# Spacers of 32 bytes between the input weight tiles of a fused attention and two-MoE kernel

## The chip, the cores and the metric

One NeuronCore of a Trainium2 chip runs the whole kernel. The metric is the device time of one execution in microseconds; before the change the median of 3 runs is 587.91 us (587.55 to 588.61). A profile is one execution recorded by the hardware profiler.

## What is computed

The reference chains a decayed linear attention and two dense feed-forward layers, all in float32:

```
attn: q, k, v of (2, 8, 768, 64); per head a decay lam; blocks with a causal decay mask and a running state
x   = attn output as (1536, 512)
layer 1: h = x @ w_in (512 x 2048);  g = h * clip(h + 3, 0, 6) / 6;  x = g @ w_out (2048 x 512)
layer 2: h = x @ w_in2;  g = (a0 + a1 h + a2 h^2 + a3 h^3) / (1 + |b0||h| + |b1| h^2 + 1e-6);  out = g @ w_out2
```

q, k and v are float32, the weights arrive as float64 (two 32-bit words an element), and the output is float32 (1536, 512).

## The kernel before

**Products.** Each float32 operand of the two layers is held as a pair of fp32r tiles, a rounded high part and the rest (names end in h and l). A product is three matmuls: high by high, high by low, low by high. The weights of a layer are cut into 16 slices f of 128 hidden columns; the tokens into 3 blocks tb of 512. Slice f has four weight tiles of 2048 bytes in each partition: `wih`, `wil` (input weights, four pieces kk of 128 columns) and `woh`, `wol` (output weights). The second layer's weights overwrite the first's in the same tiles.

**Steps.** There are 96 steps s: two layers, three blocks, sixteen slices. Step s has 24 matmuls of 512 moving columns. `mm1(s)` (L226, L228, L230) makes the hidden block in the PSUM bank `hb` with 12 of them: a piece of `wih` or `wil` is the stationary operand, a piece of the activation tiles `xh` or `xl` (2048 bytes each) the moving one. `mm2(s)` (L245) adds the slice to the four accumulators `acc` with 12 more: in layer 1 pieces of `woh`, `wol` are stationary and the hidden tiles `gh`, `gl` move; in layer 2 pieces of `gh`, `gl` are stationary and `woh`, `wol` move. The order of mm1 and mm2 is the list `turns`; a step's mm2 comes two or three steps after its mm1. In the last twelve steps `gh` and `gl` live in the input weight tiles of slices 0 to 11, which are no longer needed (`g_tiles`). Every matmul has its own weight load (PEld in the profile), which runs beside the matmul ahead of it.

**Around it.** ScalarE, VectorE and GpSimd turn the weights of the next slice from float64 into the two fp32r tiles (`conv_c` to `conv_h`) and make the hidden activations (`act1`, `act2`, `act_fin`). The attention is interleaved with the first steps; its tiles lie in the pool `ap`.

**Where the tiles lie.** A pool is a stretch of each partition's SBUF and its tiles follow each other in the order of their `tile` calls. From the left end stand `const`, then `wp` with the input weights of slices 0 to 4 and the output weights of slices 0 to 8 (`w_tiles(wp, range(EARLY), range(EOUT))`), then the activations `xp`, the scratch pools `tp` and `rp`, and the hidden tiles `gp`. Behind them comes `pp` for the first loads, and when that is closed `wr` takes its place with the input weights of slices 5 to 10. From the right end stand `side`, an area of 704 bytes that nothing reads or writes (`spare`), and then `ap`; when the attention is over `wq` takes its place with the input weights of slices 11 to 15 and the output weights of slices 9 to 15. In this layout all of these weight tiles, the activation tiles and the hidden tiles begin at the same byte modulo 2048, namely 1312: `wih0` at 1312, `xh0` at 58656, `gh` at 138528, `wih5` at 154912, `wih11` at 179488, `woh9` at 199968.

Of the kernel before, what the change touches and what calls it, by code (L numbers as in the profile page):

```python
# [8 lines left out]
F32 = mybir.dt.float32  # L9
# [21 lines left out]
def fused_kernel(  # L31
# [45 lines left out]

    def w_tiles(pool, ins, outs):
        for f in ins:
            W["in", f] = [pool.tile([128, KD, 128], F32R, name=f"wi{x}{f}") for x in "hl"]  # L80
        for f in outs:
            W["out", f] = [pool.tile([128, DM], F32R, name=f"wo{x}{f}") for x in "hl"]


    side = ctx.enter_context(tc.tile_pool(name="side", bufs=1, side="right"))
    side.tile([128, 176], F32, name="spare")
    EARLY, EIN, EOUT = 5, 11, 9
    w_tiles(wp, range(EARLY), range(EOUT))
    pre = ExitStack()
    pp = pre.enter_context(tc.tile_pool(name="pp", bufs=1))  # L90
# [228 lines left out]
    with ExitStack() as actx:  # L319
# [129 lines left out]
        with tc.manual_schedule():  # L449
# [84 lines left out]
            for s in range(att_steps):  # L534
                c = CPT + s
                j = s + 3
                if s == 0:
# [21 lines left out]
                    pre.close()  # L559
                    wr = ctx.enter_context(tc.tile_pool(name="wr", bufs=1))  # L560
                    w_tiles(wr, range(EARLY, EIN), ())
                else:
                    mm1(s + 1)
# [30 lines left out]

    wq = ctx.enter_context(tc.tile_pool(name="wq", bufs=1, side="right"))
    w_tiles(wq, range(EIN, NF), range(EOUT, NF))
    W2AT = N1 - NF
    with tc.manual_schedule():
# [100 lines left out]
```

## Time and profile before

| what | value |
|---|---|
| median of 3 runs | 587.91 us |
| span of the profiled execution, first to last instruction | 586.0 us |
| PE (matmul) busy | 580.1 us, 99% of the span |
| PEld (weight load) busy | 475.4 us, 81% |
| DVE / ACT / POOL busy | 429.8 / 385.4 / 361.2 us |
| matmuls | 3117, of which 2304 belong to the 96 steps |

The profile has no other time for that execution than its span, so sums are made against 586.0 us and then carried over to the median, which lies 1.91 us higher. A matmul row's duration is latency, not rate: matmuls are pipelined and overlap. The rate is read from the distance between two starts.

### The profile page before, as it was taken

Reading aid. Unit: us, or ns where it says so; the run is one execution under the profiler, and the core shown is the slowest. Engines: PE = TensorE matmul, PEld = TensorE weight load, DVE = VectorE, ACT = ScalarE, POOL = GpSimd, SP = SyncE. Lnnn points to the kernel's source line nnn. Section 1 sums busy time; section 2 is a strip of 40 time slices with the busy share of each in tenths; the row PEclk is TensorE's granted clock in tenths of the full one; section 3 lists DMA queues with packets and bytes.
Section 4 is the critical chain, followed back from the end, with each engine's and each line's share of the span. In section 5 each row is a group of like instructions: output and inputs, shape, how many; then the busy total and the mean of one; then the engine's idle time right before and its main releaser. Section 6 shows DMA issues by size and latency. Waiting matters only on the chain.

```text
span 586.0 us, 8507 instructions
## 1 busy us (share of the span) xinstructions
PE 580.1 (99%) x3117; PEld 475.4 (81%) x3117; DVE 429.8 (73%) x478; ACT 385.4 (66%) x650; POOL 361.2 (62%) x290
## 2 busy tenths in 40 slices
PE   8999999999999999999999999999999999999997
PEld 6777787888888888888888888888888888888885
DVE  6797676887211012688888999999998888999991
ACT  3686656786322223677778888888876677877771
POOL 3665757566221222476667778788776767777771
PEclk9999999999999999999999999999999999999999
DMA  9998673553000000456563001000100000100001
GB/s 184 258 263 225 160 229 126 161 162 107 1 0 1 0 1 1 165 194 182 177 196 128 2 0 37 1 1 1 73 1 0 1 1 1 72 1 0 2 1 72
DMA packets 61674, 46.69 MB, mean 80 GB/s; under 512 B 39488, under 2 KB 56128, under 8 KB 61632
## 3 DMA queue, kind: packets, MB, share of 16 engines
q1 hardware_dynamic: 61344, 46.02, 27.8%
q8 instruction: 24, 0.39, 0.3%
q10 hardware_dynamic: 288, 0.14, 0.1%
q14 instruction: 18, 0.15, 0.1%
HBM read 43.00 MB, written 3.15 MB: 79 GB/s over the span
## 4 chain that ended last, share of the span: by engine, by line
PE 96%; SPq 2%; DMA 1%; issue 0%; DVE 0%; ACT 0%
PE acc L245 45%; PE hb L226 15%; PE hb L228 15%; PE hb L230 15%; SPq L348 2%; DMA vn<-in_v_dram 1%; PE Y L391 1%; PE X L424 1%; PE Y L424 1%; PE X L413 1%; PE X L391 1%; PE hb L418 1%; PE Y L369 1%; PE X L364 1%; PE acc L391 0%; PE acc L418 0%
## 5 line engine op out<-in xcount | busy, mean ns | idle before, releaser
L314 DVE RECIPROCAL Y<-tb 128x512 f32<-128x512 f32 x48 | 161.3, 3361 | 1.6
L291 POOL TENSOR_TENSOR gl<-td,gh 128x512 fp32r<-128x512 f32 x84 | 109.1, 1298 | 82.4 <-ACT gh L290 82.4
L226 PE MATMUL hb<-xh,wih 128*128 128x512 f32 x384 | 103.8, 392 | 0.0
L228 PE MATMUL hb<-xh,wil 128*128 128x512 f32 x384 | 102.7, 389 | 0.0
L230 PE MATMUL hb<-xl,wih 128*128 128x512 f32 x384 | 102.7, 389 | 0.0
L305 POOL TENSOR_TENSOR tc<-ta,tc 128x512 f32<-128x512 f32 x48 | 62.3, 1297 | 55.0 <-ACT tc L302 55.0
L281 DVE SCALAR_TENSOR_TENSOR td<-tc,hb 128x512 f32<-128x512 f32 x48 | 32.8, 684 | 79.8 <-ACT tc L278 79.8
L230 PEld LDWEIGHTS hb<-xl,wih 128*128 128x128 f32 x384 | 72.1, 188 | 15.1
L228 PEld LDWEIGHTS hb<-xh,wil 128*128 128x128 f32 x384 | 72.1, 188 | 15.1
L226 PEld LDWEIGHTS hb<-xh,wih 128*128 128x128 f32 x384 | 71.4, 188 | 15.9 <-issue 1.4
L245 PE MATMUL acc<-gh,woh 128*128 128x512 f32 x192 | 76.1, 396 | 0.0
L245 PE MATMUL acc<-gl,woh 128*128 128x512 f32 x192 | 74.9, 390 | 0.0
L245 PE MATMUL acc<-gh,wol 128*128 128x512 f32 x192 | 74.8, 390 | 0.0
L278 ACT ACTIVATE tc<-hb,c 128x512 f32<-128x512 f32 x48 | 32.8, 684 | 60.6 <-PE hb L230 60.4
L290 ACT CAST gh<-td 128x512 fp32r<-128x512 f32 x84 | 52.0, 619 | 25.4 <-DVE td L281 13.5
L306 POOL TENSOR_TENSOR td<-td,tc 128x512 f32<-128x512 f32 x48 | 64.4, 1341 | 3.8
L218 POOL TENSOR_TENSOR wil<-ta,wih 128x512 fp32r<-128x512 f32 x32 | 41.5, 1296 | 28.2 <-ACT wih L217 28.2
L299 ACT ACTIVATE X<-hb,b_sb 128x512 f32<-128x512 f32 x48 | 31.8, 662 | 39.0 <-PE hb L230 36.2
L245 PE MATMUL acc<-woh,gh 128*128 128x512 f32 x144 | 56.0, 389 | 0.0
L245 PE MATMUL acc<-wol,gh 128*128 128x512 f32 x144 | 56.0, 389 | 0.0
L245 PE MATMUL acc<-woh,gl 128*128 128x512 f32 x144 | 56.0, 389 | 0.0
L218 POOL TENSOR_TENSOR wol<-tb,woh 128x512 fp32r<-128x512 f32 x29 | 38.4, 1326 | 14.0 <-ACT woh L217 13.4
(124 smaller groups left out, 1013.2 us busy)
## 6 DMA issues: line engine op xcount, KB each, us to landing
raw<-in_moe_w_in_dram SPq DMA_DIRECT2D x32, 512.0 KB, 4.1
raw<-in_moe_w_out_dram SPq DMA_DIRECT2D x32, 512.0 KB, 4.7
qn<-in_q_dram SPq DMA_DIRECT2D x24, 128.0 KB, 3.8
kn<-in_k_dram SPq DMA_DIRECT2D x24, 128.0 KB, 3.6
vn<-in_v_dram SPq DMA_DIRECT2D x12, 256.0 KB, 5.1
out_dram<-raw SPq DMA_DIRECT2D x11, 256.0 KB, 2.2
out_dram<-raw ACTq DMA_DIRECT2D x1, 128.0 KB, 1.8
out_dram<-raw SPq DMA_DIRECT2D x1, 128.0 KB, 1.8
```

Of the source, the lines that this page charges most:

```text
L218: nc.gpsimd.tensor_tensor(lo, x, hi.bitcast(F32), op=ALU.subtract)
L226: nc.tensor.matmul(h, lhsT=ih[:, kk, :], rhs=xh[tb][:, kk, :], start=kk == 0, stop=False)
L228: nc.tensor.matmul(h, lhsT=il[:, kk, :], rhs=xh[tb][:, kk, :], start=False, stop=False)
L230: nc.tensor.matmul(h, lhsT=ih[:, kk, :], rhs=xl[tb][:, kk, :], start=False, stop=kk == KD - 1)
L245: nc.tensor.matmul(acc[d], lhsT=l, rhs=r, start=st and i == 0, stop=sp and i == 2)
L278: nc.scalar.activation(t, h, AF.Relu, bias=c3)
L281: nc.vector.scalar_tensor_tensor(out=g, in0=t, scalar=6.0, in1=h, op0=ALU.min, op1=ALU.mult)
L290: nc.scalar.copy(gh, g)
L291: nc.gpsimd.tensor_tensor(gl, g, gh.bitcast(F32), op=ALU.subtract)
L305: nc.gpsimd.tensor_tensor(b1, h2, b1, op=ALU.mult)
L306: nc.gpsimd.tensor_tensor(a1, a1, b1, op=ALU.add)
L314: nc.vector.reciprocal(Y, q1)
```

## The change

```diff
@@ -77,13 +77,13 @@
     def w_tiles(pool, ins, outs):
         for f in ins:
+            if f:
+                pool.tile([128, 8], F32, name=f"step{f}")
             W["in", f] = [pool.tile([128, KD, 128], F32R, name=f"wi{x}{f}") for x in "hl"]
         for f in outs:
             W["out", f] = [pool.tile([128, DM], F32R, name=f"wo{x}{f}") for x in "hl"]
 
 
-    side = ctx.enter_context(tc.tile_pool(name="side", bufs=1, side="right"))
-    side.tile([128, 176], F32, name="spare")
     EARLY, EIN, EOUT = 5, 11, 9
```

Ahead of each slice's pair of input weight tiles but the first, an unused tile of 8 float32 (32 bytes) is placed; nothing reads or writes it. The area of 704 bytes at the right end is gone. No instruction is added, removed or moved: on all five engines the changed program has the same instructions in the same order with the same waits; only addresses differ. The addresses of the changed program, as starts modulo 2048 against those of `xh`, `xl`, `gh` and `gl` (all at 1440 now, 128 higher than before, since four spacers stand ahead of them):

| tiles | start against activations, bytes |
|---|---|
| input weights f = 0, 1, 2, 3, 4 | -128, -96, -64, -32, 0 |
| input weights f = 5, 6, 7, 8, 9, 10 | +32, +64, +96, +128, +160, +192 |
| input weights f = 11, 12, 13, 14, 15 | +448, +480, +512, +544, +576 |
| output weights f = 0 to 8 | 0 |
| output weights f = 9 to 15 | +576 |

Before the change every entry of this table is 0.

## Rows read from the trace of the kernel before

**Rows 1.** The page: the span and its first part, busy time by engine.
```profile
span 586.0 us, 8507 instructions
...
PE 580.1 (99%) x3117; PEld 475.4 (81%) x3117; DVE 429.8 (73%) x478; ACT 385.4 (66%) x650; POOL 361.2 (62%) x290
```

**Rows 2.** The waits of PE: who it waited for, total us, times, longest.
```profile
PE Y L477 <- DVE warm L467: 1.2, 1, 1.2
PE acc L418 <- DMA vn<-in_v_dram: 0.6, 1, 0.6
PE acc L391 <- ACT kT L370: 0.2, 1, 0.2
```

**Rows 3.** Busy time by stage; columns as in the first line.
```profile
core 0: us, PE busy (x) PEld busy (x) DVE busy (x) ACT busy (x) POOL busy (x), PEclk, DMA share, GB/s
...
26.30:103.30 77.00, 77.00 (x697) 60.78 (x698) 59.02 (x98) 52.39 (x100) 50.60 (x43) 1.00 0.75 201
103.30:329.30 226.00, 226.00 (x997) 187.12 (x998) 125.66 (x183) 129.89 (x227) 110.42 (x86) 1.00 0.31 96
329.30:490.00 160.70, 160.70 (x710) 133.07 (x709) 150.65 (x106) 125.03 (x197) 122.45 (x95) 1.00 0.03 11
```

**Rows 4.** PE in order of time, a step of layer 1: start us, us, what.
```profile
301.90 0.39 PE L245 MATMUL acc<-gh,woh 128*128 128x512 f32 x1
...
304.62 1.07 PE L226 MATMUL hb<-xh,wih 128*128 128x512 f32 x4
305.53 1.07 PE L228 MATMUL hb<-xh,wil 128*128 128x512 f32 x4
306.44 1.07 PE L230 MATMUL hb<-xl,wih 128*128 128x512 f32 x4
307.34 0.39 PE L245 MATMUL acc<-gh,woh 128*128 128x512 f32 x1
```

**Rows 5.** PE in order of time, a step of layer 2.
```profile
494.34 0.39 PE L245 MATMUL acc<-woh,gh 128*128 128x512 f32 x1
...
497.06 1.07 PE L226 MATMUL hb<-xh,wih 128*128 128x512 f32 x4
...
499.78 0.39 PE L245 MATMUL acc<-woh,gh 128*128 128x512 f32 x1
```

**Rows 6.** PE in order of time among the attention, first stretch.
```profile
31.27 1.19 PE L226 MATMUL hb<-xh,wih 128*128 128x512 f32 x4
32.30 1.08 PE L228 MATMUL hb<-xh,wil 128*128 128x512 f32 x4
33.21 1.07 PE L230 MATMUL hb<-xl,wih 128*128 128x512 f32 x4
34.12 1.07 PE L226 MATMUL hb<-xh,wih 128*128 128x512 f32 x4
```

**Rows 7.** PE in order of time among the attention, later stretches.
```profile
40.96 0.40 PE L245 MATMUL acc<-gl,woh 128*128 128x512 f32 x1
41.20 0.39 PE L245 MATMUL acc<-gh,woh 128*128 128x512 f32 x1
...
44.65 1.08 PE L228 MATMUL hb<-xh,wil 128*128 128x512 f32 x4
45.57 1.08 PE L230 MATMUL hb<-xl,wih 128*128 128x512 f32 x4
46.49 0.38 PE L364 MATMUL X<-ident,qn 128*128 128x128 f32 x2
```

**Rows 8.** PE in order of time, bf16 matmuls at the start.
```profile
6.20 0.38 PE L477 MATMUL Y<-warm 128*128 128x512 bf16 x1
6.42 0.60 PE L369 MATMUL hb<-ident,kn 128*128 128x128 f32 x4
```

**Rows 9.** Line 226's instructions: duration ns min/median/max, first and last start us.
```profile
L226 PEld LDWEIGHTS hb<-xh,wih x384: 186/188/189, 26.2 to 563.5; 128*128 128x128 f32 x192
L226 PE MATMUL hb<-xh,wih x384: 389/389/499, 26.2 to 563.7; 128*128 128x512 f32 x192
```

## The prediction

> **What bounds the kernel now.** I read the first part of the page first: the matmul engine is busy 580.1 of 586.0 us [rows 1]. Then the waits: PE waited 2.0 us in the whole execution, 1.2 + 0.6 + 0.2, each of them once [rows 2]. By stage, PE is busy for every one of the 77.0, 226.0 and 160.7 us between 26.3 and 490.0 us, at a granted clock of 1.00, which is the level of 2.4 GHz, while VectorE, ScalarE and GpSimd each have idle time in all three [rows 3]. So no engine and no transfer holds PE up; the time is the number of matmuls times the distance between their starts, and only a change of that distance can move it.
>
> That distance is the thing to measure. Between 301.90 and 307.34 us one step of layer 1 passes, 24 matmuls of 512 columns in 5.44 us, 226.7 ns each; the three groups of mm1 take 0.91, 0.91 and 0.90 us for four matmuls, so mm1 and mm2 run at one rate [rows 4]. In layer 2, where stationary and moving operands have changed places in mm2, the step from 494.34 to 499.78 us takes 5.44 us again [rows 5]. The steps hold 96 x 24 = 2304 matmuls; at 226.7 ns they are 522 us, nine tenths of the span.
>
> Two observations say that 226.7 ns is not simply the length of the operand. First, 512 columns at one a cycle of 2.4 GHz are 213.3 ns, and a bf16 matmul of the same size at the start has 0.22 us to the next start [rows 8]. So there are some 7 to 13 ns in each fp32r matmul that the columns do not explain, up to 2304 x 13.3 = 31 us in all. Second, the distance is not quite constant. Just after attention work it is longer: from 44.65 to 46.49 us eight matmuls of mm1 take 1.84 us, 230 ns each, and one in mm2 takes 0.24 us to two digits [rows 7]. It then settles: from 32.30 to 33.21 us it is 227.5 ns, and from 33.21 to 34.12 us 227.5 ns again to that precision [rows 6], and in the undisturbed stages it stays at 226.7. Something in how the weight load and the moving stream meet depends on how they stand to each other in time. Whether it also depends on their addresses, no row shows: every weight, activation and hidden tile of the steps begins at the same byte modulo 2048.
>
> **The change part by part.** No instruction is added or removed and no wait changes, so nothing is queued behind anything new. The spacers are neither read nor written: zero instructions, 0 us. The order of the DMAs and their sizes is the same; that their destinations lie 128 to 704 bytes further on could matter only to landing times, and after 26.3 us PE waits for no transfer [rows 2, 3]. The operands of ScalarE, VectorE and GpSimd move too; a few per cent more on any of them would go into idle time of 18 us in 77, 96 in 226 or 10 in 161 on the busiest of them [rows 3], so that is priced at nothing, and the cover is thinnest in layer 2, where VectorE has 10.05 us over some 30 steps, about 0.34 us a step.
>
> What is left is the address relation of the two reads of PE. It changes for these matmuls: in mm1 all slices but f = 4, so 90 of 96 steps with 12 matmuls, 1080; in mm2 the slices 9 to 15, 42 steps with 12, 504; and in the last twelve steps, where the hidden tiles lie in input weight tiles, four more (slices 4 to 7) with 12, 48. That is 1632 of 2304. The effect on one of them is not shown by a row of before, and I bound it from both sides. The best case is the bare column time, 213.3 ns, 13.3 less than now; the nearest measured row on that side is the bf16 matmul at 0.22 us, 7 ns less. The worst case is the 0.24 us of the disturbed mm2, 13 ns more; the nearest group on that side is the 230 ns after attention, 3.3 ns more. In the sum these are 1632 x 13.3 = 21.8 us less, 1632 x 7 = 11.4 us less, 1632 x 13 = 21.2 us more and 1632 x 3.3 = 5.4 us more. The value I take for the forecast is 0, for two reasons that rows give. The steady distance is the same whichever tiles stand against each other: pieces kk of one weight tile lie 512 bytes apart, and mm1 and mm2 and both layers pair different tiles in different regions, yet all come out at 226.7 ns [rows 4, 5]; so a dependence could only be on an offset smaller than 512 bytes. And the weight load itself takes 186 to 189 ns over all 384 instances of line 226, those after attention work among them [rows 9]; a load that collided with the stream more in one case than in another would be expected to spread further. The sum is then 586.0 + 0 = 586.0 us for the profiled execution, and with the 1.91 us that the median lies above it, 587.9 us.
>
> Here a page can be weighed. The rows show two distances for the same operands, 226.7 and 230 ns [rows 4, 7]. The Trainium skill (SBUF — State Buffer, Who interferes with whom) gives the matrix engine two independent read ports, one for the moving operand and one for weight loads, and says that it never waits on anyone. By that rule addresses play no part, the change is worth 0, and the time is 587.9 us; the trace agrees in the constancy of the undisturbed stages and does not agree in the disturbed ones, which the rule leaves unexplained.
>
> **The rivals.** *Slower: the settled state is lost.* The steady 226.7 ns is reached only after some matmuls at 230 ns or more; if it rests on the two streams starting at the same offset, slices at other offsets settle at another value, or are thrown out of it at each border between mm1 and mm2, where the offset jumps in the changed layout by up to 576 bytes and never did before. For it: nearly all of the disturbed distances are above the steady one [rows 6, 7], so another relation is more likely worse than better. Against it: the constancy named above. The price is the 3.3 ns: 1080 x 3.3 = 3.6 us if mm1 alone suffers, 591.5 us, and 5.4 us for all 1632, 593.3 us; with the 0.24 us row it would be 609. It decides as soon as the mean distance over the 1632 rises by 0.7 ns (1.2 us).
>
> *Faster: the equal offset is what costs the extra.* If the surplus over the columns is the two reads meeting in the same place because they begin at the same place, other offsets remove it, wholly or in part. For it: the surplus exists and is in each matmul [rows 4, 8]. Against it: bf16 matmuls also read both operands from one tile at one offset, and their surplus is smaller [rows 8]. At 7 ns for the 1080 of mm1 the gain is 7.6 us, 580.4 us; for all 1632 it is 11.4 us, 576.5 us; at the bare column time 566.1 us.
>
> The Trainium skill (TensorE: Matmul & The Clock Gate, Back-to-back issue gap) puts a stream of 512 columns at 512/2.4 + 2.5 = 215.8 ns. The bf16 row agrees and the fp32r rows do not; if offsets brought the 1632 matmuls down to it, the estimate would be 1632 x 10.9 = 17.8 us less, 570.1 us.
>
> *The change does less than it says.* Slice 4 keeps offset 0, and so do the output weights 0 to 8, since the activation tiles are shifted along. With an effect that depends only on whether a start is a multiple of 64 bytes, the even and the odd slices would part and half of mm1 would move: 540 x 3.3 = 1.8 us or 540 x 7 = 3.8 us, 589.7 or 584.1 us. These sit inside the two rivals and have no chance of their own.
>
> **How the numbers follow.** A measurement of this kernel can tell about 0.2%, 1.2 us, from no change. No dependence on the address: 0.38, 587.9 us, 586.7 to 589.1. The settled state lost: 0.34, 589.1 to 609, mostly 590 to 596. The equal offset was the cost: 0.28, 566 to 586.7, mostly 576 to 586. These are faster 0.28, same 0.38, slower 0.34. The likeliest single case gives the time. A range of 8 in 10 must reach into both rivals: from 577, which leaves out the case in which nearly every changed matmul gains fully (about 0.09), to 596, which leaves out losses of over 5 ns a matmul (about 0.1). The likeliest case alone has 587.0 to 588.9.
>
> **What would show it.** In the changed profile, the distance of 24 matmuls in a step decides everything: 5.44 us for every slice f means no dependence; a distance that differs from step to step in a pattern with period 16, equal in the three blocks and both layers, shows the address at work, and its sign by slice says which rival holds, with slice 4 as the control that must stay at 0.91 us for four matmuls of mm1. PE must still be 99% busy with the same waits. The prediction is wrong if the span leaves 584.8 to 587.2 us; my account of it is wrong if PE shows new waits, because then the time went through another engine and not through the distance of the matmuls.

## The result, and the profile after

The changed kernel takes 596.79 us (median of 4 runs, 596.49 to 597.09) against 587.89 us for the kernel before on the same chip: a ratio of 1.015, 95% interval 1.0136 to 1.0165, slower by 8.9 us. The forecast was 587.9 us with a range from 577 to 596; the time lies above it, on the side of the slower rival.

| what | before | after |
|---|---|---|
| median | 587.89 us | 596.79 us |
| span of the profiled execution | 586.0 us | 595.1 us |
| PE busy | 580.1 us | 589.7 us |
| PEld busy | 475.4 us | 475.9 us |

The page of the changed kernel, its span and busy time by engine; it answers to [rows 1]:

```profile
span 595.1 us, 8507 instructions
...
PE 589.7 (99%) x3117; PEld 475.9 (80%) x3117; DVE 431.3 (72%) x478; ACT 385.5 (65%) x650; POOL 361.5 (61%) x290
```

The instructions are the same in number; the span grew by 9.1 us and PE's busy time by 9.6 us, while the busy time of the others moved by 1.5 us at most. The waits of PE in the changed kernel, which answer to [rows 2], have not grown:

```profile
PE Y L477 <- DVE warm L467: 1.3, 1, 1.3
PE acc L391 <- ACT kT L370: 0.2, 1, 0.2
PE acc L418 <- DMA vn<-in_v_dram: 0.2, 1, 0.2
```

So no other engine and no transfer holds PE up. What changed is the distance between matmuls. PE in order of time in layer 1 of the changed kernel, mm1 of slices 4, 5, 6 and 11, each with the start of what follows it where it is shown; the rows answer to [rows 4]:

```profile
253.18 1.07 PE L226 MATMUL hb<-xh,wih 128*128 128x512 f32 x4
254.09 1.07 PE L228 MATMUL hb<-xh,wil 128*128 128x512 f32 x4
254.99 1.07 PE L230 MATMUL hb<-xl,wih 128*128 128x512 f32 x4
255.90 0.39 PE L245 MATMUL acc<-gh,woh 128*128 128x512 f32 x1
...
258.63 1.09 PE L226 MATMUL hb<-xh,wih 128*128 128x512 f32 x4
259.55 1.10 PE L228 MATMUL hb<-xh,wil 128*128 128x512 f32 x4
260.49 1.10 PE L230 MATMUL hb<-xl,wih 128*128 128x512 f32 x4
...
264.14 1.10 PE L226 MATMUL hb<-xh,wih 128*128 128x512 f32 x4
265.08 1.09 PE L228 MATMUL hb<-xh,wil 128*128 128x512 f32 x4
266.01 1.09 PE L230 MATMUL hb<-xl,wih 128*128 128x512 f32 x4
...
291.82 1.08 PE L226 MATMUL hb<-xh,wih 128*128 128x512 f32 x4
292.73 1.08 PE L228 MATMUL hb<-xh,wil 128*128 128x512 f32 x4
293.65 1.07 PE L230 MATMUL hb<-xl,wih 128*128 128x512 f32 x4
```

Slice 4, whose weights still stand at offset 0, takes 2.72 us for its twelve matmuls (253.18 to 255.90), as before. Slice 5 at +32 takes 0.94 us for four (259.55 to 260.49), slice 6 at +64 takes 0.93 (265.08 to 266.01), slice 11 at +448 takes 0.92 (292.73 to 293.65), against 0.91 at offset 0. The mean distance of the twelve, from the starts in the trace, repeats by slice. Here it stands for the second block of layer 1 beside the offset:

```
slice   0     1     2     3     4     5     6     7     8     9     10    11    12    13    14    15
offset  -128  -96   -64   -32   0     +32   +64   +96   +128  +160  +192  +448  +480  +512  +544  +576
mm1 ns  231.9 233.3 229.4 232.7 226.7 232.8 233.2 234.0 233.0 233.2 229.0 228.8 233.1 229.2 233.1 233.3
```

The third block of layer 1 has the same numbers within 0.1 ns. Summed over the starts of both traces, mm1 has become 5.5 us longer and mm2 3.7 us, together the 9.1 us of the span to rounding. In mm2, the slices 9 to 15 (+576 in layer 1) carry 2.8 us and the slices 0 to 8 carry 0.9 us. Of this 0.9, slices 4 to 7 of the last block, whose hidden tiles lie in input weight tiles, carry 0.25 us; the other 0.6 us fall on matmuls that kept offset 0: the first of them after a disturbed mm1 still run at 224 to 237 ns before they settle at 226.7.

### The profile page after: what moved, and what is told of

Read it like the earlier page. It is cut to its first block, busy times and chain, and to the rows that moved or that the text cites. A ratio compares the mean times of both kernels' runs of the same rounds, so it can differ in the third digit from the quotient of the medians.

```text
span 595.1 us, 8507 instructions
## 1 busy us (share of the span) xinstructions
PE 589.7 (99%) x3117; PEld 475.9 (80%) x3117; DVE 431.3 (72%) x478; ACT 385.5 (65%) x650; POOL 361.5 (61%) x290
## 4 chain that ended last, share of the span: by engine, by line
PE 96%; SPq 2%; DMA 1%; issue 0%; DVE 0%; ACT 0%
PE acc L245 45%; PE hb L226 15%; PE hb L228 15%; PE hb L230 15%; SPq L348 2%; DMA vn<-in_v_dram 1%; PE Y L391 1%; PE X L424 1%; PE Y L424 1%; PE X L413 1%; PE X L391 1%; PE hb L418 1%; PE X L364 1%; PE Y L369 1%; PE acc L391 0%; PE acc L418 0%
## 5 line engine op out<-in xcount | busy, mean ns | idle before, releaser
L226 PE MATMUL hb<-xh,wih 128*128 128x512 f32 x384 | 105.6, 396 | 0.0
L228 PE MATMUL hb<-xh,wil 128*128 128x512 f32 x384 | 104.7, 394 | 0.0
L230 PE MATMUL hb<-xl,wih 128*128 128x512 f32 x384 | 104.4, 393 | 0.0
```

The lines of the kernel that those rows point to most:

```text
L226: nc.tensor.matmul(h, lhsT=ih[:, kk, :], rhs=xh[tb][:, kk, :], start=kk == 0, stop=False)
L228: nc.tensor.matmul(h, lhsT=il[:, kk, :], rhs=xh[tb][:, kk, :], start=False, stop=False)
L230: nc.tensor.matmul(h, lhsT=ih[:, kk, :], rhs=xl[tb][:, kk, :], start=False, stop=kk == KD - 1)
```

## The experiments

Three theories stood against each other. **A:** each offset between the stationary and the moving start has a steady distance of its own. **B:** only the jump of the offset from one group of matmuls to the next costs. **C:** something else that moved, such as the tiles at the right end, is the cause.

### map1: the offset alone

A kernel of its own, which leaves out the computation and issues groups of N = 32 matmuls; `m` and `d` are the moving and the stationary offset in bytes, `c` the stationary columns (the branch for bf16 is left out here):

```
for g, (kind, m, d, c) in enumerate(plan()):
    ...
        l, r = (far if kind == "far" else sta)[:, d // 4 : d // 4 + c], mov[:, m // 4 : m // 4 + 512]
    for i in range(N):
        nc.tensor.matmul(acc[g % 2][0:c, :], lhsT=l, rhs=r, start=True, stop=True)
```

> This kernel leaves out the whole computation: it issues groups of 32 matmuls of 512 fp32r columns with one stationary and one moving tile, and from group to group only the byte offset of the stationary start against the moving start changes (0 to 1024 in steps of 32, then 4 to 60 in steps of 4, then both starts shifted together by 32, 64 and 256, then fewer stationary columns, a stationary tile 98 KB further on, and bf16). Theory A, each offset has a steady distance of its own that repeats every 512 bytes: 226.7 ns at 0, 512 and 1024, about 229 at 192 and 448, 232 to 234 at 32, 64, 96, 128 and 160, the same again from 512 to 1024, and 226.7 when both starts move together. Theory B, only the jump of the offset between groups of matmuls costs: after at most 10 matmuls every group is at 226.7 ns. Theory C, the address relation is not the cause (other engines' addresses are): all groups at 226.7 from the start.

Measured, as mean distance of the last 20 matmuls of a group in ns; the values of 256 to 480, 512 to 736 and 768 to 992 are those of 0 to 224 within 0.1:

```
offset   0      32     64     96     128    160    192    224    256
ns       226.7  233.4  233.4  234.1  232.4  233.2  228.9  233.4  226.7
```

Busy time by stretch in map1, where each stretch reaches from the first start of one group of 32 to that of the next (the columns are stretch, us, PE busy and the matmuls that reach into it, granted clock, DMA share, GB/s). The offsets are 64, 96, 128, 160, 192, 224, 256:

```profile
26.05:33.52 7.47, 7.47 (x34) 1.00 0.01 2
33.52:41.00 7.48, 7.48 (x33) 1.00 0.00 0
41.00:48.43 7.43, 7.43 (x33) 1.00 0.00 0
48.43:55.90 7.47, 7.47 (x34) 1.00 0.00 0
55.90:63.23 7.33, 7.33 (x34) 1.00 0.01 2
63.23:70.69 7.46, 7.46 (x33) 1.00 0.00 0
70.69:77.95 7.26, 7.26 (x33) 1.00 0.00 0
```

7.26 us over 32 are 226.9 ns, 7.47 are 233.4. With no other engine at work and nothing but the offset changed, the distances of the changed kernel's slices come out within 0.7 ns: 192 and 448 at 228.9, 32 and 64 at 233.4. Slice 13 alone is off by more: at 512 map1 has 226.7, and the kernel has 229.2, because the first seven of its twelve matmuls, which follow mm2 at +576, run at 224 to 236 ns before they settle. Theories B and C fall: at none of the offsets between 0 and 256 in this table does a group return to 226.7 in 32 matmuls. A holds, but not the period that it was given: it expected 512 bytes, and 256 came out. Offset 0 in the table is its first group once settled. Each offset has its own repeating pattern: at 192 the distances run 226, 229, 232, at 64 they alternate between 231 and 236, at 0 they are constant.

The other groups: both starts moved together by 32, 64 or 256 bytes settle at 226.7, and so does a stationary tile 98 KB further on, so the address itself and the region do not count. Steps of 4 bytes between 4 and 60 give 230.0 to 235.0. With 64 and 32 stationary columns at offset 0 the distance is 230.3 and 231.7, no shorter. In bf16 the distance is 215.8 at offsets 0, 64, 128 and 256 alike (three matmul records are missing there). The groups at 0 and 128, 32 matmuls in 6.91 and 6.90 us:

```profile
419.21:426.12 6.91, 6.91 (x32) 1.00 0.00 0
433.03:439.93 6.90, 6.90 (x33) 1.00 0.00 0
```

### sparedrop and leftonly: half of the change each

sparedrop removes the spare area alone:

```diff
-    side = ctx.enter_context(tc.tile_pool(name="side", bufs=1, side="right"))
-    side.tile([128, 176], F32, name="spare")
```

> The kernel before without the spare area and without spacers: input weights 11 to 15 and output weights 9 to 15 lie at +704 bytes, all others at 0. Theory A (offset modulo 512, 704 is 192): mm1 of slices 11 to 15 at 229.0 ns in place of 226.7 (360 matmuls, +0.8 us), mm2 of slices 9 to 15 at 229.0 in layer 1 (252, +0.6 us) and at the value of -192 in layer 2, which no run has shown, 0 to 7 ns (0 to +1.8 us), and some settling after each return to 0: 589.4 to 591.9 us, with slices 0 to 10 at 226.7. Theory B (jumps cost): 4 jumps a block, each with some 10 matmuls at +4.5 ns, 24 x 45 ns: +1.1 us, 589 us, and every slice back at 226.7 by the end of a step. Theory C (the shift of the right side's other tiles by 704 bytes is what slows): a slowdown that does not sit in slices 9 to 15.

Measured 591.22 us (590.91 to 592.46) against 588.75 us for the kernel before on that chip, a ratio of 1.0048, interval 1.003 to 1.0065: 2.5 us. PE in order of time, mm1 of slice 10 (offset 0) and 11 (+704) in layer 1, with the line numbers of this kernel, two lower:

```profile
196.74 1.07 PE L226 MATMUL hb<-xh,wil 128*128 128x512 f32 x4
197.65 1.07 PE L228 MATMUL hb<-xl,wih 128*128 128x512 f32 x4
...
202.19 1.08 PE L226 MATMUL hb<-xh,wil 128*128 128x512 f32 x4
203.11 1.07 PE L228 MATMUL hb<-xl,wih 128*128 128x512 f32 x4
```

0.91 us against 0.92 for four. Over all twelve, slices 11 to 15 are at 228.8 to 228.9 in layer 1, and mm2 of slices 9 to 15 at 228.8 to 229.0: the value that map1 has at 192 and 704. In layer 2 the hidden tile is the stationary operand, the offset of slices 9 to 15 is -704, which is 64 modulo 256, and mm2 stands at 233.3: the value at 64. The expectation had left this value open. Outside the attention, slices 0 to 10 have 226.7 in mm1 except right behind the disturbed ones in layer 2 (230.2 in slice 0, 228.3 in 1 to 3). There mm1 of slices 11 to 15 too is between its own value and that of mm2 beside it, 229.0 to 233.1. But for this settling, the cost sits where the offset is.

leftonly keeps the spacers of slices 1 to 10 and leaves 64 bytes of the spare area:

```diff
-            if f:
+            if 0 < f < 11:
...
+    side.tile([128, 16], F32, name="spare")
```

> The changed kernel with the spacers of slices 1 to 10 alone and a spare area of 64 bytes, which puts input weights 11 to 15 and output weights 9 to 15 at +512. Theory A: these are back at 226.7 ns; slices 0 to 10 keep what they have in the changed kernel, +3.75 us in mm1 and +0.9 us of settling in mm2: about 592.5 us. Theory B: the offset jumps at nearly every border between mm1 and mm2 of slices 0 to 10 and at none in the rest: much the same, 592 to 593 us, but with distances that fall to 226.7 within a group of 12. Theory C (right side alone): the slowdown is unlike that of the changed kernel, since the right side lies elsewhere.

Measured 593.18 us (593.10 to 593.31) against the same 588.75 us, a ratio of 1.0077, interval 1.006 to 1.0093: 4.4 us. In mm1, slices 11 to 15 at +512 are back at 226.7 in every block but the last. PE in order of time, slice 11 in the third block of layer 1, twelve matmuls in 2.72 us:

```profile
290.37 1.07 PE L228 MATMUL hb<-xh,wih 128*128 128x512 f32 x4
291.27 1.07 PE L230 MATMUL hb<-xh,wil 128*128 128x512 f32 x4
292.18 1.07 PE L232 MATMUL hb<-xl,wih 128*128 128x512 f32 x4
293.09 0.39 PE L247 MATMUL acc<-gh,woh 128*128 128x512 f32 x1
```

Slices 0 to 10 have the numbers of the changed kernel within about 1 ns; from the starts, their mm1 is 3.7 us longer and mm2 of 0 to 8 0.9 us. The expectation had left out mm2 of slices 9 to 15, 0.9 us more: half of it in the last block, the rest in mm2 of slices 12 to 15, which follows the disturbed mm1 of the next block's first slices (227 to 231 ns).

The two medians, 2.5 and 4.4 us, do not add up to 8.9, because the kernel before took 0.9 us longer on that chip (588.75 us; its 7 runs lie between 587.70 and 589.33) than on the chip of the result (587.89 us). From the starts, against one and the same trace of the kernel before, mm1 and mm2 are 3.6 us longer in sparedrop and 5.7 us in leftonly, 9.3 us together against 9.1: the halves add up.

### uniform32 and uniform256: one offset for all, in the whole kernel

The kernel before with its first weight pool behind the hidden tiles and a filler ahead of it, 32 or 256 bytes, taken from the spare area (shown for 32):

```diff
-    wp = ctx.enter_context(tc.tile_pool(name="wp", bufs=1))
     xp = ctx.enter_context(tc.tile_pool(name="xp", bufs=1))
...
     gp = ctx.enter_context(tc.tile_pool(name="gp", bufs=LAG2 + 1))
+    wp = ctx.enter_context(tc.tile_pool(name="wp", bufs=1))
+    wp.tile([128, 8], F32, name="shift")
...
-    side.tile([128, 176], F32, name="spare")
+    side.tile([128, 168], F32, name="spare")
```

> The kernel before with the pool of the first weight tiles behind the hidden tiles and 32 bytes of filler ahead of it, the spare area 32 bytes smaller: every weight tile stands at +32 against every activation and hidden tile, and the offset jumps nowhere between mm1 and mm2 of layer 1. Theory A: mm1 and mm2 of all slices at 233.35 ns (map1 at 32 and at 224), 6.7 ns more: outside the attention stretch and the last twelve mm2, which pair input weight tiles with output weight tiles at offset 0, some 1030 matmuls of mm1 and 920 of mm2, +13.0 us, and about +0.5 us in the attention stretch: 601 to 602.5 us. Theory B (jumps cost): no jumps, 588 to 590 us.

Measured 601.17 us (601.04 to 601.25) against 588.24 us, a ratio of 1.022, interval 1.0205 to 1.0235. PE in order of time, mm1 of two steps running in layer 1 (lines one higher):

```profile
237.97 1.09 PE L227 MATMUL hb<-xh,wih 128*128 128x512 f32 x4
238.91 1.09 PE L229 MATMUL hb<-xh,wil 128*128 128x512 f32 x4
239.84 1.09 PE L231 MATMUL hb<-xl,wih 128*128 128x512 f32 x4
240.77 0.40 PE L246 MATMUL acc<-gh,woh 128*128 128x512 f32 x1
...
243.57 1.09 PE L227 MATMUL hb<-xh,wih 128*128 128x512 f32 x4
```

A step of 24 matmuls takes 5.60 us (237.97 to 243.57), 233.3 ns each in mm1 and mm2 alike, with no jump of the offset between them in layer 1. This is theory A at its plainest.

> The same with 256 bytes of filler: every weight tile at +256. Theory A: 256 is the period, 226.7 ns everywhere, 587 to 589 us, although every address of the weights, of the activations and of the attention's tiles has changed. Rival, the address itself (a region, the order of the pools) matters: a time other than that of the kernel before.

Measured 588.04 us (587.29 to 588.58 in 10 runs) against 588.24 us, a ratio of 0.9994, interval 0.9985 to 1.0004. The same two places of a step:

```profile
240.24 1.07 PE L227 MATMUL hb<-xh,wih 128*128 128x512 f32 x4
241.15 1.07 PE L229 MATMUL hb<-xh,wil 128*128 128x512 f32 x4
...
245.68 1.07 PE L227 MATMUL hb<-xh,wih 128*128 128x512 f32 x4
```

5.44 us again. Every weight has another address than before and another start against the activations, by a whole period, and the time is that of the kernel before.

### map2 and map3: is there a better offset, and what meets what

map2 has the matmuls of map1 at offsets in steps of 4 bytes, and then with fewer moving columns:

```
l, r = sta[:, d // 4 : d // 4 + 128], mov[:, m // 4 : m // 4 + c]
```

> Leaves out the whole computation, as map1; groups of 24 matmuls. Offsets 64 to 252 in steps of 4 bytes; then the moving start moved on by 32, 64, 128 and 192 with the stationary one at 0; then 384, 256 and 128 moving columns at offsets 0 and 64. Theory A (steady distance by offset, period 256 bytes): no offset goes below the 226.7 ns of offset 0, the values lie between 228 and 236; the moved moving start gives the value of 256 minus the shift: 233.4, 228.9, 232.4 and 233.4. Rival, offset 0 is not special: some of the offsets that are no multiple of 32 come out under 226 ns, down to the 215.8 of bf16. For fewer columns: if the surplus belongs to the weight load of each matmul, the 13.3 ns over the column time stay (173.3, 120.0 and 66.7 ns at offset 0); if it belongs to the stream of columns, it shrinks with them (170, 113.3 and 56.7 ns), unless the load itself, at some 107 ns, is the bound.

No offset falls below 226.7 ns. Offset 0 is not alone at it: 120, 144, 156, 204 and 252 settle there too, 132 after some twelve matmuls; the rest lie between 228.4 and 237.4, where theory A had said 228 to 236 for all. The moved moving starts came out as expected within 0.2 ns (233.4, 228.8, 232.6 and 233.3). Busy time by stretch for 384 columns at offsets 0 and 64, then 256 columns at 0 and 64, each one group of 24 (columns as in map1):

```profile
271.94:276.10 4.16, 4.16 (x26) 1.00 0.00 0
276.10:280.33 4.23, 4.23 (x25) 1.00 0.00 0
280.33:283.20 2.87, 2.87 (x26) 1.00 0.00 0
283.20:286.03 2.83, 2.83 (x27) 1.00 0.00 0
```

Settled, 384 columns have 173.4 ns at offset 0 and 176.7 at 64: 128 columns fewer take 53.3 ns off at offset 0, which is their time at one a cycle of 2.4 GHz, so the surplus stays about 13.3 ns, and what offset 64 adds falls from 6.7 to 3.3. With 256 columns the distance is 119.8 and 117.8, so offset 64 is now the better one; with 128 columns it is 111.7 at both. At offset 0 a fixed surplus of about 13 ns fits down to 256 columns; the ranking of the two offsets is the same at 512 and 384 columns and turns at 256.

map3 changes the steps with which the operands are read:

```
l = sta[:, o : o + 127 * st + 1 : st] if st else sta[:, o : o + 1].to_broadcast([128, 128])
r = mov[:, 0 : 511 * mt + 1 : mt] if mt else mov[:, 0:1].to_broadcast([128, 512])
```

> Leaves out the whole computation, as map1; groups of 24 matmuls of 512 columns. The stationary operand is read with steps of 2, 4 and 3 columns at offsets 0 to 224, then the moving one with a step of 2, then the stationary one as one column repeated 128 times (a single address a partition) and the moving one as one column repeated 512 times, each at offsets 0 and 64. Theory A1 (the addresses of the two reads meet while they run through SBUF): the map over offsets changes with the step, and where either operand stays at one address the offset makes no difference; if the meeting is the whole of the surplus, the repeated column comes down to some 216 ns, the distance of bf16. Theory A2 (only the two start addresses matter): the same map as at step 1, 226.7 at 0 and 228.9 to 234 elsewhere, whatever the step. If a step comes out under 226.7 ns at some offset, weights laid out with that step would make a kernel faster than both, by up to 2304 x 10.9 ns.

Busy time by stretch in map3, each one group of 24 (columns as in map1): the stationary column repeated at offsets 0 and 64, then the moving column repeated at offsets 0 and 64.

```profile
216.93:222.51 5.58, 5.58 (x25) 1.00 0.00 0
222.51:228.07 5.56, 5.56 (x25) 1.00 0.00 0
228.07:233.32 5.25, 5.25 (x25) 1.00 0.01 3
233.32:238.57 5.25, 5.25 (x26) 1.00 0.00 0
```

Settled, these are 231.7, 231.7, 218.7 and 218.7 ns. As soon as one operand stays at one address, offsets 0 and 64 give the same distance, while with both operands read through they are 6.7 ns apart. The two start addresses alone therefore do not set the distance, and A2 falls; the runs fit A1, though that the two reads meet in SBUF is a reading of these times and was not seen as such. With the moving operand at one address 2.9 ns are left over bf16's 215.8; with the stationary one at one address the distance is 231.7, so a load whose address stands still does not remove the surplus. At a step of 2 the map is another one (230.0 to 233.8), at a step of 3 it is 233.2 to 240.0 and at a step of 4 233.3 to 239.7; there the offsets 0, 4, 8 and 12 all give 235.0 with one pattern of distances while 16 gives 233.4. A moving operand with a step of 2 takes 453 ns. But for the one repeated moving column, which is no use to a product, nothing that was tried with 512 fp32r columns comes under 226.7 ns, so these runs point to no version that beats the kernel before, and none was made.

## Why the prediction was wrong

**What bounds the kernel: right.** PE is 99% busy after the change as before, its waits are the same, and the whole difference lies in the distance between matmuls, which the prediction named as the only thing that could move. The fillers, the DMAs and the other engines cost nothing, as priced: uniform256 moves the addresses of all of them and takes the same time.

**Which matmuls change: right in the main.** The 1632 matmuls named carry 8.5 of the 9.1 us, 5.2 ns each; the other 0.6 us fall on matmuls that kept offset 0 and come right behind disturbed ones. The offset of 512 in mm1 of slice 13 is a whole number of periods and costs nothing of its own. The control named for the reading, slice 4, stayed at 2.72 us for twelve. The pattern has a period of 16 slices, as was said it would if the address counted; in layer 2 it differs by up to 1.6 ns in slices 11 to 15 of the first two blocks, where mm2 beside them stands at another offset.

**The step that failed is the value 0 for the price of one of them.** It rested on two readings. The first was that pairs 512 bytes apart and tiles in different regions all stand at 226.7 [rows 4, 5], from which the text itself drew that only an offset smaller than 512 could count. That is what the spacers make; the reading ruled out nothing that the change does, and it was taken for evidence of constancy all the same. The runs showed a period of 256 bytes and a price inside it of 2.2 to 7.4 ns at the multiples of 32. The second was that the weight load takes 186 to 189 ns in all cases [rows 9]. It still takes 188 ns in the changed kernel and in map1 at nearly all offsets, while the distance between matmuls changes: the price does not show in the mean duration of the load. From the page of the changed kernel:

```profile
L226 PEld LDWEIGHTS hb<-xh,wih 128*128 128x128 f32 x384 | 71.4, 188 | 17.3 <-issue 1.2
```

The column time misled on the other side, too: the bf16 row [rows 8] is no sign of what an fp32r matmul could reach by its address, for no offset came below 226.7.

**The slower rival had the mechanism and too small a size.** It said that the steady value rests on the equal start, that other offsets settle at other values, and that the distances among the attention [rows 6, 7] tell more likely of something worse. All of that the runs bear out. Its price, 3.3 ns from the 230 ns after attention work [rows 7], is the mean of a passing state on its way to offset 0's value; the steady values of most other offsets are higher. So it put mm1 at 3.6 us and all 1632 at 5.4, where 5.5 and 8.5 were measured, and the range left out losses of over 5 ns a matmul, which is where the 5.2 ns lie. With map1's values for each slice the sum is: mm1, the sixteen slices' surplus adds up to 78.5 ns, times 12 matmuls and 6 blocks, 5.7 us (measured 5.5); mm2 of slices 9 to 15 in layer 1, at 64, 252 x 6.7 ns = 1.7 us (measured 1.6); in the first two blocks of layer 2, where the offset is -576 or 192 modulo 256, 168 x 2.2 ns = 0.4 us (measured 0.7, with settling); in the last twelve steps, whose offsets run through the table once more, 59.9 ns x 12 = 0.7 us (measured 0.7). Together 8.4 us, and with the 0.6 us of settling in mm2 at offset 0, 9.1 us, the 9.1 us of the span. The rival's other half, being thrown out at each border, is the settling, the 0.6 us above all: present, and the small part.

**The faster rival fell.** Its doubt, that bf16 also reads both operands from one offset and has a smaller surplus, was the right one.

**Two reads that never wait.** The matmul distance depends on the relation of the two addresses, 226.7 at 0 and 233.4 at 32 in map1, with no other engine at work. The Trainium skill (SBUF — State Buffer, Who interferes with whom) has the matrix engine's two read ports independent and the engine never waiting on anyone; by that rule the change was worth 0. The measurement decides against that value for fp32r operands, while the bf16 groups of map1, 215.8 ns at the four offsets tried, agree with it.

**What stays open.** Why the distance depends on the offset with a period of 256 bytes, why a second group of offsets (120, 144, 156, 204, 252) is as good as 0, and what the 10.9 ns between 226.7 and bf16's 215.8 are, of which 8 go when the moving operand stays at one address. No run separates these.

## What to carry to other kernels

Where PE is the bound and runs fp32r matmuls of 512 columns back to back, measure the distance from start to start by tile, and keep every stationary tile at the same byte modulo 256 as the moving tile that it runs against; a filler that kept this cost nothing (uniform256), and those that undid it cost up to 7.4 ns of 226.7 a matmul here. For other lengths measure again: at 256 columns offset 64 was better than 0. An observation that cannot vary along the axis of the change (all offsets multiples of 512 bytes) is no evidence that the axis does not matter: give the bound from the rows of disturbed states its full weight then. A kernel that holds only the disputed instruction and sweeps one number settles such a question in one run.

## What the runs showed of the hardware that was not expected

- The distance of fp32r matmuls of 512 columns depends on the offset between the stationary and the moving start with a period of 256 bytes: 226.7 ns at 0, 228.9 at 192, 232.4 to 234.1 at the other multiples of 32 (map1); in bf16 it is 215.8 at 0, 64, 128 and 256.
- A load of 32 stationary columns is itself shorter, 108 ns against 188 for 128 columns in map1, and does not shorten the distance (231.7 ns against 226.7 at offset 0).
- With a stationary step of four fp32r, offsets 0, 4, 8 and 12 are one case and 16 is another. The Trainium skill (SBUF — State Buffer, Door 1: The DMA port swizzle) has SBUF in lines of 16 bytes; the trace agrees, 235.0 ns four times and then 233.4.
- A moving operand read with a step of two fp32r takes 453 ns for 512 columns, twice the distance.
